# First batch's transposed q and k: where the four-way interleave is undone in the copy out of PSUM

## Chip, cores and metric

The kernel runs on one NeuronCore of a Trainium2 chip. The metric is device time of one execution in microseconds; of the kernel before, 13 runs gave a median of 309.38 us (307.45 to 310.54).

## What is computed

q, k and v have the shape (8 batches, 8 heads, 576 positions, 64). Per batch and head, retention: scores q k^T / 8, multiplied by a decay that is zero above the diagonal, times v. The heads are laid side by side (4608 tokens x 512) and go through a feed-forward block with a hard-swish, 512 to 2048 to 512.

```python
scores = scale * np.matmul(q, k.transpose(0, 1, 3, 2))
Dmat = np.where(rel >= 0, gamma[:, None, None] ** rel[None, :, :], 0.0)
attn = np.matmul(scores * Dmat[None], v)
x = np.ascontiguousarray(attn.transpose(0, 2, 1, 3)).reshape(B * S, H * D)
h = x @ w_in
out = (h * np.clip(h + 3.0, 0.0, 6.0) / 6.0) @ w_out
```

The decay is folded into q, k and v when they are cast to fp16 (tables `tq` and `tkv`), so that the scores need only a mask of zeros and ones.

## The kernel before

**Tiling.** A batch is cut into four chunks of 128 positions and a tail of 64; two tails make one more chunk. For each chunk: load q, k, v (`load`), cast them to fp16 with the decay (`cast`, L172), transpose q and k (`xpose`, by DMA, or `xpose_pe`, on TensorE), scores and mask (`ret1`: matmuls L277, VectorE's mask L284), then products with v, with the running state, and the new state (`ret2`: L300, L306, L325; ScalarE copies the result to `xt`, L330, and the state to fp16, L336). Four chunks fill `xt` for one batch. Then the up-projection (`up` L369, `up_half` L385) with the hard-swish (ScalarE L352, VectorE L357) and the down-projection: plain for batch 0 (`down_plain_part`, L412), by seven products of half size for the others (`product`, L483, with sums by VectorE, L447). Weights are loaded by `wload` (L539, L543) and cast by `wcast` (VectorE L555, ScalarE L557, GpSimd L559); `tbuild` (L572) makes differences of w_out.

**Order.** The order of the work is written out by hand in the string `PROGRAM`. Each engine runs its instructions in this order, and waits by semaphore for what others deliver. All loads and stores are issued by SP, in the same order; the DMA transposes are issued by ScalarE. The beginning reads

```
H19 L0.0 L0.1 L1.0 L1.1 C0.0v C0.1v V0 W0.0 W0.1 V1 V2 V3 W0.2 W0.3 c0.2g
C1.0v X0.0s W0.7 X0.1s X1.0s C1.1v X1.1s s0.4 K0v w0.0s s1 c1.2g K1v o0
```

H is 19 matmuls on zeros. L loads a half of the heads of q (0) or k (1); C casts it on VectorE; X transposes it, with the copy on ScalarE (the s at the end); V loads one chunk of v; W and w load and cast weights; c casts (on GpSimd, where the letter is g); s, o are `ret1`, `ret2`; K makes k back from its transpose; the second number of `s0.4` asks for four more matmuls on zeros.

**The first batch.** Its 512 positions take a way of their own. `load0` puts four neighbouring positions on one partition (partition p holds positions 4p to 4p + 3, 1024 bytes for each head), `cast0` (L208) casts them into `qk0["16"]` with r = 0 to 3 as the place among the four, and `xpose0` transposes, for each pair of heads a and each r, a block of 128 x 128 on TensorE (L223). A PSUM tile `tp` thus holds [pair, r, p]: positions r, 4 + r, 8 + r and so on. The attention needs them in order, 4p + r, and a copy (`copy`, ScalarE, L216) moves the tile into `wout16`, which serves as storage until w_out is cast into it. There are four such copies of 128 x 1024 fp16 elements: q heads 0 to 3, q heads 4 to 7, k heads 0 to 3, k heads 4 to 7. The scores of a chunk use all four: the first four matmuls of `ret1` use the first and the third copy, the last four the second and the fourth. `kback` transposes k of these chunks back (L237, copied by VectorE, L214), and `ret2` uses it for the state. The PSUM tiles of `xpose0` come from the four buffers with the tag `mm`, which the projections use later.

The functions around the change, and what calls them:

Of the kernel before, what the change touches and what calls it, by code (L numbers as in the profile page):

```python
# [83 lines left out]
def kernel(  # L84
# [39 lines left out]
    wout16 = const.tile([P, NFC, DM], FP16)  # L124
# [87 lines left out]
    def copy(eng, dst, src):  # L212
        if eng == "v":
            nc.vector.tensor_copy(dst, src)  # L214
        else:
            nc.scalar.copy(dst, src)  # L216

    def xpose0(ix, hh, eng):
        tp = psum.tile([P, 2, 4, P], FP16, tag="mm", bufs=4, name="tp")
        for a in range(2):  # L220
            for r in range(4):
                n0 = (2 * hh + a) * P
                nc.tensor.transpose(tp[:, a, r, :],  # L223
                                    qk0["16"][:, ix, r, n0:n0 + P], ident)
        p0 = 4 * ix + 2 * hh
        dst = wout16[:, p0:p0 + 2, :].rearrange("z a (p r) -> z a r p", r=4)
        copy(eng, dst, tp)
        if ix == 1 and hh == 1:
            for t in range(NC4):
                qkTs[(0, 0, t)] = wout16[:, 0:8, t * P:(t + 1) * P]  # L230
# [378 lines left out]
    for h in range(H):  # L609
        z = h % 2  # L610
# [17 lines left out]
    def act(w):  # L628
# [6 lines left out]
        elif kind == "C":  # L635
            cast0(*n, ENG[e])
        elif kind == "X":
            xpose0(*n, e)
        elif kind == "K":
            kback(*n, e)  # L640
# [65 lines left out]
```

## Time and profile before

The profiled execution took 310.37 us; its span is 308.2 us at a mean granted TensorE clock of 0.981.

| | us |
|---|---|
| median of 13 runs | 309.38 |
| profiled execution, span | 310.37, 308.2 |
| TensorE busy | 292.8 |
| VectorE, ScalarE, GpSimd busy | 241.9, 147.0, 108.8 |
| the four copies of `xpose0` (L216) | 9.3 in all |
| first start of L216, start of the second half of the first scores | 8.61, 17.92 |
| DMA, read and written | 36.70 MB, 9.44 MB |

An engine's row in a table of groups gives the busy time of the group, the mean duration of one instruction in ns, and then how long the engine sat idle just before these instructions and what it waited for. In the timeline the columns are start, duration, engine, line, operation, output and input, count, and in brackets the idle time before. In the chain of waits they are start, duration, and whose work the end hung on. In a row of the windows the stretch and its length come first, then each engine's busy time and instruction count (TensorE, its weight loads, VectorE, ScalarE, GpSimd), then the granted clock, the DMA share and the GB/s.

### The profile page before, as it was taken

How to read it: one execution, taken by the hardware profiler on the slowest of the kernel's cores; microseconds unless marked ns; L12 is line 12 of the kernel's file. 1: busy time of each engine (PE TensorE's matmuls, PEld its weight loads, DVE VectorE, ACT ScalarE, POOL GpSimd, SP SyncE). 2: the span in 40 equal slices, each digit the busy share in tenths (PEclk: the TensorE clock that was granted, in tenths of full speed). 3: DMA queues.
4: the chain of work that ended last, by engine and by line, in shares of the span. 5: the costliest groups of instructions: out<-in, count | busy, mean ns of one | idle time of the engine just before them, and what ended most of it. 6: DMA issues, size and time to landing. Idle time of an engine off the chain costs nothing.

```text
span 308.2 us, 7125 instructions
## 1 busy us (share of the span) xinstructions
PE 292.8 (95%) x2887; PEld 199.8 (65%) x2887; DVE 241.9 (78%) x335; ACT 147.0 (48%) x259; POOL 108.8 (35%) x120
## 2 busy tenths in 40 slices
PE   8369999989999999999999999999999999999995
PEld 3257445568788888746864686468655874685584
DVE  6346785988987989889877977898599767966963
ACT  2855762457235753366327522763277226505610
POOL 3164364894092655474375143332500000000000
PEclk9859999999999999999999999999999999999999
DMA  7999999999999999999999999989601430014003
GB/s 239 294 291 394 264 278 219 201 193 188 239 177 176 196 241 233 220 202 228 247 194 199 278 212 204 220 171 161 150 3 34 36 121 17 0 36 103 2 0 136
DMA packets 149728, 53.93 MB, mean 175 GB/s; under 512 B 134848, under 2 KB 145088, under 8 KB 149696
## 3 DMA queue, kind: packets, MB, share of 16 engines
q1 hardware_dynamic: 120128, 46.15, 68.2%
q10 hardware_dynamic: 29568, 7.34, 17.3%
q8 instruction: 22, 0.36, 0.5%
q14 instruction: 10, 0.08, 0.1%
HBM read 36.70 MB, written 9.44 MB: 150 GB/s over the span
## 4 chain that ended last, share of the span: by engine, by line
PE 85%; DVE 9%; ACT 4%; issue 1%; DVEq 0%
PE ph L369 29%; PE accB L483 9%; PE accC L483 9%; PE accA L483 9%; PE ph L385 8%; PE accD L483 5%; PE sc L277 4%; PE xp L300 4%; ACT wout L216 3%; PE xp L252 2%; PE po L412 2%; DVE g L357 2%; PE xp L306 2%; DVE tmat L572 2%; PE state L325 1%
## 5 line engine op out<-in xcount | busy, mean ns | idle before, releaser
L352 ACT ACTIVATE u<-ph 128x512 f32<-128x512 f32 x144 | 84.6, 597 | 67.2 <-PE ph L369 42.9
L357 DVE SCALAR_TENSOR_TENSOR g<-u,ph 128x512 f16<-128x512 f32 x144 | 95.3, 684 | 23.0 <-ACT u L352 21.4
L369 PE MATMUL ph<-xt,win 128*128 128x512 f16 x368 | 82.6, 379 | 0.2
L369 PEld LDWEIGHTS <-win 128*128 128x128 f16 x432 | 41.2, 98 | 48.3 <-DVE win L555 0.6
L483 PEld LDWEIGHTS <-ss 128*128 128x128 f16 x512 | 48.8, 98 | 7.1 <-DVE ss L447 1.1
L172 POOL TENSOR_TENSOR v<-st,tkv 128x512 f16<-128x512 f32 x31 | 35.2, 1142 | 46.4 <-DMA st<-in_v_dram 21.7
L284 DVE TENSOR_TENSOR at<-sc,mask 128x1024 f16<-128x1024 f32 x32 | 39.0, 1218 | 13.3 <-PE sc L277 13.2
L172 POOL TENSOR_TENSOR qk<-st,tq 128x512 f16<-128x512 f32 x29 | 31.8, 1096 | 41.2 <-PE state L325 24.0
L483 PEld LDWEIGHTS <-g 128*128 128x128 f16 x384 | 36.9, 98 | 5.5
L172 POOL TENSOR_TENSOR qk<-st,tkv 128x512 f16<-128x512 f32 x28 | 31.4, 1124 | 9.8 <-DMA st<-in_k_dram 9.0
L330 ACT ACTIVATE xt<-xp 128x512 f16<-128x512 f32 x32 | 19.1, 597 | 32.9 <-PE xp L306 20.6
L385 PE MATMUL ph<-xt,win 128*128 128x256 f16 x288 | 33.5, 273 | 1.1 <-DVE osb L420 1.1
L483 PE MATMUL accB<-tmat,ss 128*128 128x256 f16 x256 | 30.6, 273 | 0.2 <-DVE ss L447 0.2
L483 PE MATMUL accA<-wout,g 128*128 128x256 f16 x256 | 30.6, 273 | 0.0
L385 PEld LDWEIGHTS <-win 128*128 128x128 f16 x288 | 27.4, 98 | 4.9 <-issue 1.3
L447 DVE TENSOR_TENSOR ss<-g 128x1024 f16<-128x1024 f16 (+1 forms) x30 | 22.5, 754 | 0.3
L300 PE MATMUL xp<-at,v 128*64 128x128 f16 x288 | 20.3, 228 | 0.0
L300 PEld LDWEIGHTS <-v 128*64 128x64 f16 x288 | 14.2, 111 | 6.7 <-issue 3.4
L336 ACT CAST s<-state 64x256 f16<-64x256 f32 x48 | 17.3, 361 | 0.5
L503 ACT COPY osb<-accA 128x512 f32<-128x512 f32 x8 | 4.7, 586 | 23.9 <-PE accA L483 23.9
L412 PE MATMUL po<-wout,g 128*128 128x512 f16 x64 | 15.3, 379 | 0.6 <-DVE g L357 0.5
L483 PE MATMUL accC<-tmat,ss 128*128 128x256 f16 x128 | 15.4, 273 | 0.0
(87 smaller groups left out, 278.0 us busy)
## 6 DMA issues: line engine op xcount, KB each, us to landing
st<-in_v_dram SPq DMA_DIRECT2D x32, 256.0 KB, 6.0
out_dram<-osb SPq DMA_DIRECT2D x32, 256.0 KB, 3.7
st<-in_q_dram SPq DMA_DIRECT2D x28, 256.0 KB, 5.4
st<-in_k_dram SPq DMA_DIRECT2D x28, 256.0 KB, 5.4
wst<-in_moe_w_in_dram SPq DMA_DIRECT2D x4, 512.0 KB, 6.7
tmat<-in_moe_w_in_dram SPq DMA_DIRECT2D x4, 512.0 KB, 9.0
wst<-in_moe_w_out_dram SPq DMA_DIRECT2D x4, 512.0 KB, 10.5
g<-in_moe_w_out_dram SPq DMA_DIRECT2D x4, 512.0 KB, 8.1
```

Source lines behind the costliest of these rows:

```text
L172: eng.tensor_tensor(out=dst, in0=st[:, ix, :, :], in1=tab.unsqueeze(2).to_broadcast([P, H, D]), op=ALU.mult)
L284: nc.vector.tensor_tensor(out=at.rearrange("p z a i -> p (z a) i"), in0=sc.rearrange("p z a i -> p (z a) i"), in1=m[:, :].unsqueeze(1).to_ ...
L300: nc.tensor.matmul(xp[rows[z], p, :], vt[:, 2 * p + z, :], at[:, z, p, :], start=(p == 0), stop=False, skip_group_check=True)
L330: nc.scalar.activation(xts[b][:, :, t * P:(t + 1) * P], xp, ACTF.Copy, scale=0.125)
L336: nc.scalar.copy(s16[rows[z], :, rows[z]], sp[rows[z], :, :])
L352: nc.scalar.activation(u, ph, ACTF.Relu, bias=0.5, scale=1.0 / 6.0)
L357: nc.vector.scalar_tensor_tensor(out=dst, in0=uv, scalar=1.0, in1=pv, op0=ALU.min, op1=ALU.mult)
L369: nc.tensor.matmul(ph, win16[:, m, P * fc:P * fc + P], xt[:, m, :], start=(m == 0), stop=(m == NCC - 1))
L385: nc.tensor.matmul(ph[:, 256 * j:256 * j + 256], win16[:, m, P * fc:P * fc + P], xt[:, m, cs], start=(m == 0 and j == 0), stop=(m == NCC - 1),
L412: nc.tensor.matmul(po, g[:, fc, P * mc:P * mc + P], wout16[:, fc, :], start=(fc == 0), stop=(fc == NFC - 1))
L447: nc.vector.tensor_tensor(out=dst, in0=a, in1=c, op=op)
L483: nc.tensor.matmul(ps[:, m, :], lhs(fc, m), rhs[:, fc, :], start=(first and fc == 0 and m == 0), stop=(fc == HF - 1 and m == 1), skip_grou ...
```

## The change

The copy still moves the same 1024 elements a partition, on the same engine, at the same place in the program. Before, it read PSUM in the order in which it lies there, [pair, r, p], and wrote to SBUF with a step of four elements. After, it writes SBUF in the order in which that lies, [pair, p, r], and reads PSUM with r innermost, four elements that lie 128 elements apart.

```diff
         p0 = 4 * ix + 2 * hh
-        dst = wout16[:, p0:p0 + 2, :].rearrange("z a (p r) -> z a r p", r=4)
-        copy(eng, dst, tp)
+        dst = wout16[:, p0:p0 + 2, :].rearrange("z a (p r) -> z a p r", r=4)
+        copy(eng, dst, tp.rearrange("z a r p -> z a p r"))
```

## Prediction

> **What bounds the kernel now.** I read the page first, then the chain of waits in order of time, then the groups with shapes kept apart, then the timelines of TensorE and GpSimd over the first 30 us and of both TensorE and VectorE around 62 us, and last the windows for the granted clock.
>
> ```profile
> PE 292.8 (95%) x2887; PEld 199.8 (65%) x2887; DVE 241.9 (78%) x335; ACT 147.0 (48%) x259; POOL 108.8 (35%) x120
> PEclk9859999999999999999999999999999999999999
> ```
>
> TensorE is busy for 292.8 of 308.2 us. A change on another engine can win only from the 15.4 us in which TensorE idles, or from matmuls that run at a low granted clock, which the second row shows only in slices 2 and 3 (a slice is 7.7 us). The chain of waits names one large piece of that:
>
> ```profile
> 8.13 0.46 PE tp L223 x8
> 8.59 0.02 issue
> 8.61 9.26 ACT wout L216 x4
> 17.87 0.05 issue
> 17.92 0.41 PE sc L277 x4
> ```
>
> From 8.61 to 17.87 us the end hangs on four ScalarE copies in a row and on nothing else: the very copies that are changed. Then the scores of the first chunk start. TensorE's timeline shows when each copy could have started and what the wait costs:
>
> ```profile
> 9.89 0.62 PE L223 MATMUL tp<-ident,g 128*128 128x128 f16 x8 [0.87 <-DVE g L208]
> 11.39 0.62 PE L223 MATMUL tp<-ident,g 128*128 128x128 f16 x8 [0.88 <-DVE g L208]
> 11.85 0.39 PE L252 MATMUL sc<-zero 128*128 128x128 f16 x4
> 15.64 0.40 PE L277 MATMUL sc<-wout 64*128 64x128 f16 x4 [3.41 <-ACT wout L216]
> 17.92 0.40 PE L277 MATMUL sc<-wout 64*128 64x128 f16 x4 [1.88 <-ACT wout L216]
> ```
>
> The last transposes are done at 12.01 (11.39 + 0.62); the data is ready, and 3.41 + 1.88 = 5.29 us of idle TensorE are waits on L216. The groups give the price of such a copy, and of its nearest relative:
>
> ```profile
> L216 ACT COPY wout<-tp 128x1024 f16<-128x1024 f16 x4 | 9.3, 2512 | 6.0 <-PE tp L223 6.0
> L267 ACT COPY qkT<-tp 128x1024 f16<-128x1024 f16 x1 | 1.0, 1013 | 2.9 <-PE tp L263 2.9
> ```
>
> Same engine, same 1024 fp16 elements from PSUM to SBUF; L267 is contiguous on both sides and takes 1013 ns, L216 writes with a step of four elements and takes 2512 ns. So the step on the write costs 1.5 us per copy.
>
> **The change part by part.** The four copies keep their engine, place, count and semaphores. Removed: the stepped write. Added: a stepped read, four elements 128 apart (256 bytes), 256 runs of them. No DMA, wait, buffer or instruction is added or moved, so no queue (SP's and GpSimd's included) is passed; nothing new stands behind a wait.
>
> *Price of one new copy.* No row here reads PSUM with a step. Lower bound: the contiguous 1013 ns. The nearest row with a step is L216: 1499 ns extra on 1024 jumps, 1.46 ns a jump. Its jump is 8 bytes, the new one 256, and no row says how the price grows with the length; for the bound above I let it double, an assumption: 1013 + 1024 x 2.93 = 4.0 us. I take 1013 ns: the write becomes contiguous as in L267, only the reading side differs from that row, and at 1 ns an element L267 reads no faster than one element at a time, so that it draws little from reading neighbours. Both ends stay among the cases.
>
> [...]
>
> *The copy chain.* With 1.01 us each and starts no earlier than the transposes: first 8.61 to 9.62, second to 10.6; the third waits for transposes done at 10.51 and ends at 11.6; the fourth waits for 12.01 and ends at 13.04. Before: 17.87. So the second half of the first scores comes 4.83 us earlier; the four copies lose 6 us, 1.2 of which turn into waits for the casts L208 (paced by the k loads).
>
> *Where the gain meets a load.* What follows is an alternation of TensorE, VectorE and ScalarE, which moves up as a whole until it needs something that a load sets. First such place, GpSimd's timeline:
>
> ```profile
> 20.27 1.04 POOL L559 CAST win<-wst 128x1024 f16<-128x1024 f32 x1 [2.02 <-DMA wst<-in_moe_w_in_dram]
> 21.27 1.04 POOL L172 TENSOR_TENSOR v<-st,tkv 128x512 f16<-128x512 f32 x1
> ```
>
> The cast of the fourth v ends at 22.31 whatever ScalarE does, because the cast ahead of it in GpSimd's queue waits for a load; the products of the fourth chunk (ret2) cannot start before 22.35. They started at 27.12, so the gain is capped there at 4.77 us: any more that TensorE wins before is idled away. Next, the first full up-projection (31.82) waits for the VectorE cast L555, which stands behind an activation of the chunks before; it moves with the rest. Later loads: SP was blocked 7.0 us for that L555 (a staging buffer), yet the DMA queue ran at 387 GB/s until 31.8 and sagged only to 166 and 276 GB/s in the two us after, so later loads land about 0.9 us earlier, not 4.8. I therefore checked the casts against their users at 4.8 us less: k of chunk 5 is cast by 42.0, its transposes would come at 44.2; k of chunk 6 by 48.5 against 50.7; w_out part 4 by 44.7 against 47.3. Two us of slack remain at the tightest. From 65 us on SP waits again and again for buffers that the compute frees, so loads move with it. I cost these at nothing; if a slack were gone, up to 2 us would be lost.
>
> *What may be won besides.* VectorE is full from 55 to 65 us and TensorE stalls there:
>
> ```profile
> 63.24 1.03 PE L385 MATMUL ph<-xt,win 128*128 128x256 f16 x8 [1.15 <-DVE osb L420]
> 64.44 0.40 PE L277 MATMUL sc<-qkT 64*128 64x128 f16 x8 [0.17 <-DVE qkT L265]
> ```
>
> Between 0 and 1.32 us; VectorE's work there is still paced by loads that move only 0.9, so I take 0.4.
>
> *Clock.* The windows show it:
>
> ```profile
> 12.00:13.00 1.00, 0.23 (x5) 0.06 (x1) 0.00 (x0) 1.00 (x1) 0.41 (x1) 1.00 1.20 302
> 13.00:14.00 1.00, 0.00 (x0) 0.00 (x0) 0.00 (x0) 1.00 (x2) 0.00 (x0) 0.69 1.34 229
> 23.00:24.00 1.00, 1.00 (x25) 0.80 (x26) 0.39 (x1) 0.13 (x1) 0.00 (x0) 0.69 1.04 383
> ```
>
> It is halved from 13.4 to 23.6. With less idling it may stay up, or come back sooner (about 17); that gain lies ahead of the 22.35 cap, so it is worth 0. But the wait at that cap (about 1.2 us) thins TensorE's work between 20 and 23.6 to some 60%; 1.39 us busy in the 3.4 us before 13.37 brought a halving, 2.54 us in the 3.4 us before that did not. A halving there for 3.4 us would cost 1.7 us. I take 0.
>
> Sum: 4.8 + 0.4 = 5.2 us. The profiled execution took 310.37 us (span 308.2 and 2.2 around it), 1.0 above the median; from it 305.2, from the median of 309.38, 304.2.
>
> **Rivals.**
> 1. *The read costs as much as the write did, or the change moves the same penalty.* 2.5 us per copy, chain unchanged: 309.4. For it: both are one element per jump. Against: the 8-byte and 256-byte steps are on different memories.
> 2. *Something in between*, 1.76 us a copy (the midpoint of 1013 and 2512): the four run back to back, 8.61 + 4 x 1.76 - 0.3 = 15.4, 2.5 us gained: 306.9.
> 3. *Gain made, then partly eaten* by the halved clock at 23.6: 5.2 - 1.7 = 3.5: 305.9.
> 4. *Slower: a jump in PSUM costs 2.93 ns, twice one in SBUF.* 4.0 us a copy; the last ends at 8.61 + 16.0 - 0.3 = 24.3, 6.5 us late: 315.9. It decides from 2512 ns a copy on. Nothing in the trace excludes it.
> 5. *Hidden anyway*: later waits on loads give all back, 309.4. Against it: between 26 and 100 us TensorE idles only some 2.4 us in all, with casts ready 2 us and more ahead.
>
> **How the numbers follow.** Full-rate read and gain kept: 0.52, 302.9 to 305.5 (all of the 1.32 us stall and 0.1 more at the low end; 1.3 less at the high end). Rival 3: 0.15. Rival 2: 0.11. Rivals 1 and 5: 0.09. Rival 4 and lesser slow reads: 0.13. The range 302.9 to 309.4 leaves out the slow reads, half of the ties and the fringe: 2 in 10. A measurement of this kernel tells about 0.3% (0.9 us) from no change. Faster: 0.52 + 0.15 + 0.11 = 0.78; same 0.09; slower 0.13.
>
> **What would show it.** L216 near 1.0 us, the last copy's end near 13, first scores complete by 13.4, the fourth ret2 near 22.4 with a new TensorE wait on the v cast ahead of it, the first full up-projection near 27, less idle at 62. Wrong it would be by L216 over 2.5 us; or, with L216 at 1.0, by a new TensorE wait on a load-paced cast at 35 to 60 us, or a granted clock of 0.5 after 23.6.

## The result, and the profile after

The changed kernel takes 306.31 us (median of 11 runs, 305.47 to 307.09); the kernel before took 309.55 us in the 48 runs it is set against. The ratio is 0.9893 with a 95% interval of 0.9875 to 0.9912: faster by 3.2 us, or 1.1%. The forecast was 304.2 us, range 302.9 to 309.4. The sign and the price of the copy came out as forecast; 2.0 us of the forecast gain of 5.2 is missing, and most of what follows is about where it went.

Two rows of the page, busy time and, in 40 slices of 7.6 us, the granted TensorE clock:

```profile
PE 293.7 (96%) x2887; PEld 200.4 (66%) x2887; DVE 238.8 (78%) x335; ACT 141.5 (46%) x259; POOL 108.0 (35%) x120
PEclk9969999999999999999999999999999999999999
```

TensorE does the same 2887 matmuls and the span is 304.5 us instead of 308.2, so the gain is idle time that went; one slice instead of two is at a low clock. The group of the changed copies (the same columns as before):

```profile
L216 ACT COPY wout<-tp 128x1024 f16<-128x1024 f16 x4 | 4.0, 1013 | 7.3 <-PE tp L223 7.3
```

1013 ns instead of 2512, to the nanosecond the row of L267 that the prediction took. The four copies no longer run back to back: ScalarE now sits idle for 7.3 us ahead of them and waits for transposes. The chain of waits of the kernel after over the same stretch:

```profile
2.38 8.44 DMA g<-in_k_dram
10.82 0.02 issue
10.84 1.24 DVE g L208
12.08 0.05 issue
12.12 0.64 PE tp L223 x8
12.78 1.02 ACT wout L216
13.80 0.05 issue
13.85 0.41 PE sc L277 x4
```

Where 9.26 us of copies stood, one copy of 1.02 us is left. Ahead of it stands the load of the second half of k, issued at 2.38 us and landed at 10.82: in this execution the first scores are as early as that load lets them be. TensorE's timeline of the kernel after, past that point and around 62 us of the kernel before:

```profile
13.85 0.39 PE L277 MATMUL sc<-wout 64*128 64x128 f16 x4 [0.66 <-ACT wout L216]
...
23.44 0.25 PE L300 MATMUL xp<-at,v 128*64 128x128 f16 x2
...
27.45 9.12 PE L369 MATMUL ph<-xt,win 128*128 128x512 f16 x40
...
57.45 1.91 PE L385 MATMUL ph<-xt,win 128*128 128x256 f16 x16
59.30 0.40 PE L277 MATMUL sc<-qkT 64*128 64x128 f16 x8
```

Waits on L216 were 5.29 us and are 0.66. The products of the fourth chunk (ret2) start at 23.44 with no wait in brackets, the first full up-projection at 27.45, and the waits of 1.15 and 0.17 us ahead of the scores of chunk 7 are gone.

The starts of the same work in the two profiled executions show where the lead is won and lost (s7 is the scores of chunk 7, as in the written order):

| start of, us | before | after | lead | step |
|---|---|---|---|---|
| first scores, second half | 17.92 | 13.85 | 4.07 | won 4.07 |
| products of the fourth chunk | 27.12 | 23.44 | 3.68 | lost 0.39 |
| plain down-projection, second group | 43.64 | 40.04 | 3.60 | lost 0.08 |
| s7 | 64.44 | 59.30 | 5.14 | won 1.54 |
| s8 | 78.59 | 73.45 | 5.14 | |
| s9 | 85.22 | 81.02 | 4.20 | lost 0.94 |
| s13 | 104.86 | 100.67 | 4.19 | lost 0.01 |
| s15 | 117.48 | 113.80 | 3.68 | lost 0.51 |
| end of the span | 308.2 | 304.5 | 3.7 | |

From s15 to the end both take 190.7 us. So everything happens in the first 118 us: 4.1 us are won at the copies, 1.5 us at 62 us, and about 1.9 us are given back at four places. This is one pair of executions, whose spans differ by 3.7 us where the medians differ by 3.2. The experiments are about these steps.

### The profile page after: what moved, and what is told of

The parts are those of the page before. It is cut to its first block, busy times and chain, and to the rows that moved or that the text cites. A ratio compares the mean times of both kernels' runs of the same rounds, so it can differ in the third digit from the quotient of the medians.

```text
span 304.5 us, 7125 instructions
## 1 busy us (share of the span) xinstructions
PE 293.7 (96%) x2887; PEld 200.4 (66%) x2887; DVE 238.8 (78%) x335; ACT 141.5 (46%) x259; POOL 108.0 (35%) x120
## 4 chain that ended last, share of the span: by engine, by line
PE 87%; DVE 6%; DMA 3%; ACT 2%; issue 1%; SPq 0%; DVEq 0%; ACTq 0%
PE ph L369 30%; PE accB L483 10%; PE ph L385 9%; PE accC L483 8%; PE accA L483 8%; PE accD L483 5%; PE po L412 4%; PE xp L300 4%; PE sc L277 4%; DMA g<-in_k_dram 3%; DVE g L357 3%; DVE ss L447 2%; PE xp L306 2%; PE state L325 1%; ACT u L352 1%
## 5 line engine op out<-in xcount | busy, mean ns | idle before, releaser
L172 POOL TENSOR_TENSOR v<-st,tkv 128x512 f16<-128x512 f32 x31 | 33.8, 1095 | 51.2 <-DMA st<-in_v_dram 28.6
L284 DVE TENSOR_TENSOR at<-sc,mask 128x1024 f16<-128x1024 f32 x32 | 39.0, 1218 | 8.5 <-PE sc L277 8.4
L172 POOL TENSOR_TENSOR qk<-st,tq 128x512 f16<-128x512 f32 x29 | 31.6, 1091 | 34.2 <-PE state L325 14.8
L172 POOL TENSOR_TENSOR qk<-st,tkv 128x512 f16<-128x512 f32 x28 | 32.2, 1153 | 8.4 <-DMA st<-in_k_dram 8.1
L447 DVE TENSOR_TENSOR ss<-g 128x1024 f16<-128x1024 f16 (+1 forms) x30 | 22.7, 758 | 0.3
```

The source lines that it names most:

```text
L172: eng.tensor_tensor(out=dst, in0=st[:, ix, :, :], in1=tab.unsqueeze(2).to_broadcast([P, H, D]), op=ALU.mult)
L284: nc.vector.tensor_tensor(out=at.rearrange("p z a i -> p (z a) i"), in0=sc.rearrange("p z a i -> p (z a) i"), in1=m[:, :].unsqueeze(1).to_ ...
L447: nc.vector.tensor_tensor(out=dst, in0=a, in1=c, op=op)
```

## The experiments

**The two kernels once more.** Both without an edit, one more execution each, to see how much of the table above is one execution's chance.

> The changed kernel, one more look. In its first profile the first cast of k (L208) started at 9.33 us, 0.7 us later than in the profile of before (8.61), and so did every load of the first 30 us, although nothing has changed ahead of them. If the loads' pace is a chance of the execution, the first k cast starts anywhere from 8.6 to 9.4 here and the second half of the first scores follows it by 4.5 us; if the change makes the loads late, it starts at 9.3 again.

> The kernel before, one more look, for the same question. Chance: the first k cast starts anywhere from 8.6 to 9.4, while the second half of the first scores stays at 17.9 as long as the copies run back to back from 8.6 to 8.8 (the four copies hide a late k). Rival (the change makes the loads late): the first k cast starts at 8.6 again.

After: 306.05 us, span 303.9. Before: 311.82 us, span 309.7. The first scores' second half started at 13.47 and 16.94 us. The load of k moves by itself: its first cast started at 8.32 and 8.61 us in the two profiles of before, at 9.33 and 8.71 in those of after. The four pairings of these profiles put the lead at the first scores between 3.09 and 4.45 us. In the kernel before the scores came earlier than expected (17.9) because its first transposes began at 6.98 us instead of 7.96, and the four copies at 7.62 instead of 8.61. The half clock lasted 10.2 us in the first profile of before and 17.1 us in this one, and 6.8 us in both of after; with that the spans of the second pair differ by 5.8 us. The stall ahead of s7 was in both profiles of before (20.80 and 20.79 us from the second group of the plain down-projection to s7) and in neither of after (19.26 and 19.26).

**What a step costs, by itself.** Twenty-two copies of the same 1024 elements are added behind the end of the kernel, eleven on ScalarE and the same eleven on VectorE, each on a line of its own.

```diff
+    ts_ = tp.rearrange("z a r p -> z (a r p)")
+    tj = tp.rearrange("z a r p -> z a p r")
...
+    nc.scalar.copy(xa, ts_)
+    nc.scalar.copy(xq, tj)
+    nc.scalar.copy(x4, tp)
+    nc.scalar.copy(x2, ts_)
+    nc.scalar.copy(x8, ts_)
+    nc.scalar.copy(pr, tpr)
...
+    nc.scalar.copy(xa, s1)
+    nc.scalar.copy(xq, sj)
+    nc.vector.tensor_copy(xa, ts_)
+    nc.vector.tensor_copy(xq, tj)
+    nc.vector.tensor_copy(x4, tp)
...
```

> The changed kernel with 22 copies of 1024 elements added at its end, 11 on ScalarE and the same 11 on VectorE, each on a line of its own; its time is not to be read. Theory: reading PSUM with a jump is free on ScalarE, and the price of the old copy belongs to writing single fp16 elements with a step. Then ScalarE: contiguous 1.01 us; read jumping 256 bytes 1.01; write with a step of 4 elements 2.5, of 2 and of 8 elements also about 2.5 (a half-word written alone costs the same wherever it lies); pairs of fp16 with a step 1.0; fp32 written with steps of 2 and 4 1.0. Rival: the price grows with the distance: step 2 about 1.7, step 4 2.5, step 8 more, pairs in between, and stepped fp32 dearer than contiguous fp32. [...]

Groups by line of that kernel. L698 and L709 are contiguous on both sides, L699 and L710 read PSUM with the change's jumps, L700 and L711 write every fourth fp16, L702 and L713 every eighth:

```profile
L702 ACT COPY win<-tp 128x1024 f16<-128x1024 f16 x1 | 4.7, 4681 | 0.0
L713 DVE COPY win<-tp 128x1024 f16<-128x1024 f16 x1 | 4.7, 4680 | 0.0
...
L700 ACT COPY win<-tp 128x1024 f16<-128x1024 f16 x1 | 2.4, 2420 | 0.0
L711 DVE COPY win<-tp 128x1024 f16<-128x1024 f16 x1 | 2.4, 2420 | 0.0
...
L710 DVE COPY win<-tp 128x1024 f16<-128x1024 f16 x1 | 1.2, 1224 | 0.0
...
L698 ACT COPY win<-tp 128x1024 f16<-128x1024 f16 x1 | 1.0, 1012 | 5.1 <-PE tp L681 5.1
L699 ACT COPY win<-tp 128x1024 f16<-128x1024 f16 x1 | 1.0, 1012 | 0.0
...
L709 DVE COPY win<-tp 128x1024 f16<-128x1024 f16 x1 | 0.7, 691 | 18.5 <-ACT win L708 18.5
```

| 1024 elements, ns | ScalarE | VectorE |
|---|---|---|
| PSUM to SBUF, contiguous | 1012 | 691 |
| PSUM read with jumps of 256 bytes | 1012 | 1224 |
| fp16 write, step of 2, 4, 8 elements (4, 8, 16 bytes) | 1291, 2420, 4681 | 1291, 2420, 4680 |
| fp16 write in pairs, a pair every 8 bytes | 1012 | 693 |
| fp32 write, contiguous, step of 2, 4 (8, 16 bytes) | 1012, 1055, 1951 | 1224, 1224, 1950 |
| SBUF to SBUF, contiguous and read with jumps | 1044, 1911 | 427, 1253 |

On ScalarE the jumps in PSUM cost nothing (1012 ns in L699 as in L698); VectorE's copy goes from 691 to 1224 ns with them. The stepped fp16 write costs the same on both engines (2420 ns at a step of four elements), though these differ by 1.5 times without a step (1012 and 691), which points to the receiving side and not to the engine. It nearly doubles with each doubling of the step (1291, 2420, 4681). It isn't a price per jump: pairs of fp16 at the same 8 bytes are free (1012 and 693). So the flat price that the theory expected is wrong and growth with the step, the rival, is right, but pairs are free as the theory had it.

**Half of the change.** q is copied as before, k as after.

```diff
+        if ix == 0:
+            dst = wout16[:, p0:p0 + 2, :].rearrange("z a (p r) -> z a r p", r=4)
+            copy(eng, dst, tp)
+        else:
...
```

> Half of the change: the two copies of q write with a step as before, the two of k read with a jump as after. The first two copies then take 2.5 us each, the k copies follow without a gap, and the last one ends at about 8.7 + 2 x 2.45 + 2 x 0.95 = 15.5 instead of 13.0 to 13.8 (after) and 17.9 (before). Theory that a gain at the first scores passes to the end one for one: 2.4 us better than before, so 307.1. Rival, that loads cap the gain near 3.2 us whatever the start is: nearly the whole of 3.2 us already here, 306.5. Rival, that half a gain is worth nothing because the clock or a later stall takes it: 309.

Its copies in the groups of that kernel:

```profile
L216 ACT COPY wout<-tp 128x1024 f16<-128x1024 f16 x4 | 6.5, 1774 | 6.0 <-PE tp L223 6.0
```

306.95 us, ratio 0.9899 (0.9846 to 0.9951). The mean copy is what the prediction's second rival assumed (1.76 us), and the median is near what it gave (306.9). That agreement proves little: the ratio makes it 306.4 where the kernel before takes 309.55, and its interval runs from 304.8 to 308.0. Of the three cases expected, only the last, 309, is excluded.

Against the profiled execution of the full change it is 1.21 us later at the first scores (15.06 against 13.85), but only 0.57 at the state of the fourth chunk (24.67 against 24.10), 0.29 at s7 and 0.2 at the end. In both the clock is halved for 6.83 us, but full speed is granted again at 20.05 us in it and at 20.6 in the full change, while the work stands 1.21 us later: more of it runs at full speed. In these two executions the last 1.21 us of lead at the first scores are worth 0.2 us at the end.

**The clock kept up.** More matmuls on zeros fill TensorE's waits between 8 and 18 us; the copies are the changed ones.

```diff
-C1.0v X0.0s W0.7 X0.1s X1.0s C1.1v X1.1s s0.4 K0v w0.0s s1 c1.2g K1v o0
+C1.0v X0.0s W0.7 X0.1s H4 X1.0s H3 C1.1v X1.1s s0.12 K0v H3 w0.0s s1 c1.2g K1v o0
```

> The changed kernel with more matmuls on zeros in TensorE's idle time between the transposes and before the first two chunks' scores (10 of 512 columns and 8 of 128), so that the clock is not halved between 12 and 20 us. If it works, the work from the first scores to the fourth chunk's products, 9.6 us in both profiles of after (13.85 to 23.44 in one), takes about 1.8 us less. Theory, that the loads then take over: the third quarter of the up-projection needs the cast of a w_in piece that ends at 29.2 to 30.9 us, and TensorE already comes there at 29.9 to 30.9, so the end gains 0.7 us at most: 306.0 against 306.3 for after. Rival, that the half clock is what still holds the start: 1.8 us gained, 304.5.

The mean granted clock is 1.0 in the profile, and the fourth chunk's products meet the wait that the prediction had put there. TensorE's timeline of that kernel:

```profile
21.32 0.25 PE L300 MATMUL xp<-at,v 128*64 128x128 f16 x2 [0.74 <-POOL v L172]
```

The v cast ends at 21.27 and the products start, 2.12 us ahead of the changed kernel's 23.44. But most of that isn't the clock's. The loads came earlier in this execution: the second cast of k started at 9.59 us instead of 10.84, so that the first scores were complete 1.19 us sooner (12.66 against 13.85), and the fourth v cast ended at 21.27 instead of 23.04. From these scores to the products it takes 8.66 us instead of 9.59, 0.93 less where 1.8 was expected, because the wait for the cast takes 0.74. Had the cast ended at 23.04 here too, at most 0.4 us would have been won. Whether the added matmuls have a part in the earlier loads, no run shows. In that profile the lead holds: 2.16 us at s7, 2.3 in the span (302.2). But it doesn't hold from one execution to the next: the four times are 304.66, 306.72, 307.74 and 308.63, median 307.23, ratio 0.9894 (0.9847 to 0.9942), which decides between neither of the two expectations. The clock was 0.994 or more in all four, so that what the later ones lost they lost elsewhere; only the first has a profile, and this stays open.

**The stall at 77 us.** In the changed kernel TensorE waits 0.87 us for a sum `ss` there, and in the kernel before it doesn't. VectorE's timeline of the kernel before, and then that of the kernel after, over the same work:

```profile
76.55 0.71 DVE L447 TENSOR_TENSOR ss<-g 128x1024 f16<-128x1024 f16 x1
...
77.78 1.28 DVE L572 TENSOR_TENSOR tmat<-wout 128x1024 f16<-128x1024 f16 x2
```

```profile
71.41 1.41 DVE L447 TENSOR_TENSOR ss<-g 128x1024 f16<-128x1024 f16 x1
...
73.34 1.53 DVE L572 TENSOR_TENSOR tmat<-wout 128x1024 f16<-128x1024 f16 x2
```

The same instructions took 0.95 us longer. GpSimd was idle from 76.71 to 85.43 us in the kernel before; in the kernel after it casts beside them, and TensorE waits (GpSimd's timeline before, GpSimd's after, then TensorE's after):

```profile
75.67 1.04 POOL L172 TENSOR_TENSOR v<-st,tkv 128x512 f16<-128x512 f32 x1 [0.18 <-DMA st<-in_v_dram]
85.43 1.78 POOL L172 TENSOR_TENSOR qk<-st,tq 128x512 f16<-128x512 f32 x1 [8.71 <-PE state L325]
```

```profile
70.23 2.04 POOL L172 TENSOR_TENSOR v<-st,tkv 128x512 f16<-128x512 f32 x2
72.49 1.23 POOL L172 TENSOR_TENSOR qk<-st,tq 128x512 f16<-128x512 f32 x1 [0.22 <-DMA st<-in_q_dram]
```

```profile
77.44 1.05 PE L483 MATMUL accC<-tmat,ss 128*128 128x256 f16 x8 [0.87 <-DVE ss L447]
78.70 1.92 PE L483 MATMUL accB<-tmat,ss 128*128 128x256 f16 x16 [0.21 <-DVE ss L447]
```

GpSimd's casts are paced by loads (the bracket), which did not move with the compute: the k of chunk 12 is cast at 74.45 us in the kernel before and at 74.75 in the kernel after, while the scores of chunk 8 come 5.14 us earlier. VectorE now meets casts that it did not meet before. A first attempt moves a v cast forward in GpSimd's order, out of the way:

```diff
-c9.2g l15 c10.0g c10.1g c11.0g c11.1g c10.2g x8 h1.0.4.12 h1.0.5.13 o7 x9
+c9.2g l15 c10.0g c10.1g c10.2g c11.0g c11.1g x8 h1.0.4.12 h1.0.5.13 o7 x9
```

> The changed kernel with one GpSimd cast moved: the v of the eleventh load is cast ahead of the q and k of the twelfth, which wait for their loads. In after, these casts fall on VectorE's first sum for the fast products (L447, 1.41 us instead of 0.71, at 71.4) and TensorE idles 0.87 us at 77. Theory (this collision gives back a part of the gain): L447 near 0.7 us, no wait of 0.87 at 77, 0.9 us gained: 305.4. Rival (VectorE is behind there for other reasons, or the collision only moves to its neighbour): 306.3 as after.

306.62 us, ratio 0.9891 (0.9859 to 0.9923): the collision only moved. L447 took 1.14 us, and the wait was 0.71 us.

A second moves v casts back, behind those of the next chunk:

```diff
-c9.2g l15 c10.0g c10.1g c11.0g c11.1g c10.2g x8 h1.0.4.12 h1.0.5.13 o7 x9
+c9.2g l15 c10.0g c10.1g c11.0g c11.1g x8 h1.0.4.12 h1.0.5.13 o7 x9
...
-t2 h1.1.5.13 c11.2g l16 x10 l17 c12.0g c12.1g h1.1.6.14 c12.2g h1.1.7.15
+t2 h1.1.5.13 c12.0g c12.1g c10.2g c11.2g l16 x10 l17 h1.1.6.14 c12.2g h1.1.7.15
```

> The changed kernel with the casts of v of chunks 10 and 11 put behind the casts of q and k of chunk 12 in GpSimd's order: the same work, two casts of it later. If the collision costs the time and the casts can be placed beside work that does not mind, the wait for ss at 77 us shrinks to 0.2 us and the median falls by 0.5 us or more. Rival: q of chunk 12 waits for its load, all casts behind it slide into the later sums (L447, L492) at 77 to 81 us, another wait takes the place of this one, and the median is within 0.3 us of the changed kernel or above it.

306.35 us, ratio 0.9901 (0.9867 to 0.9935). The rival was right: L572 is back at 1.28 us, but the first sum still meets a k cast (1.47 us), the two later sums are stretched too (1.12 and 1.95 us), and the waits are 1.12 and 0.94 us, more than ever; behind s9 a third follows, of 1.06 us.

A third leaves three casts out: their v and q are filled with zeros.

```diff
+        if (order.index(c), ix) in ((10, 2), (11, 2), (12, 0)):
+            eng.memset(dst, 0.0)
+            eng.tensor_tensor(out=dst[:, 0, 0:8], in0=st[:, ix, 0, 0:8],
+                              in1=tab[:, 0:1].to_broadcast([P, 8]),
+                              op=ALU.mult)
+            return
```

> The changed kernel without the three GpSimd casts that run beside VectorE's L447 and L572 from 70 to 74 us (v of chunks 10 and 11, q of chunk 12): each is replaced by a fill with zeros and a cast of 8 elements, so the work of these casts is left out. If the collision of the two engines costs the time, L447 takes 0.7 us and L572 1.28 us there, the wait for ss ahead of accC at 77 us is gone, and the median is 0.6 to 0.9 us under the changed kernel. Rival: those operations are slow for another reason, or something behind them is late in any case; then the wait stays at 0.8 us, or it goes and the median stays within 0.3 us.

Its VectorE timeline (its lines are six higher: L453 is L447, L578 is L572), GpSimd's beside it, and TensorE's:

```profile
70.84 0.69 DVE L453 TENSOR_TENSOR ss<-g 128x1024 f16<-128x1024 f16 x1
...
72.05 1.30 DVE L578 TENSOR_TENSOR tmat<-wout 128x1024 f16<-128x1024 f16 x2
...
75.35 1.13 DVE L453 TENSOR_TENSOR ss<-g 128x1024 f16<-128x1024 f16 x1
76.51 1.95 DVE L453 TENSOR_TENSOR ss<-ss,g 128x2048 f16<-128x2048 f16 x1
```

```profile
70.87 0.53 POOL L173 MEMSET v<- 128x512 f16 x1
...
74.89 1.04 POOL L178 TENSOR_TENSOR qk<-st,tkv 128x512 f16<-128x512 f32 x1 [2.09 <-DMA st<-in_k_dram]
75.89 1.49 POOL L178 TENSOR_TENSOR v<-st,tkv 128x512 f16<-128x512 f32 x1
```

```profile
76.53 1.05 PE L489 MATMUL accC<-tmat,ss 128*128 128x256 f16 x8 [0.53 <-DVE ss L453]
78.52 1.92 PE L489 MATMUL accB<-tmat,ss 128*128 128x256 f16 x16 [0.94 <-DVE ss L453]
```

With the casts gone the first sum takes 0.69 us, beside a fill, and the differences 1.30: the casts are the cause of the stretch, and the fill doesn't stretch the sum. But the next k was loaded only by 74.89 us, and its cast and the one behind it hit the two following sums (1.13 and 1.95 us). The time is 306.53 us, ratio 0.9912 (0.9882 to 0.9942): nothing was gained, against what the first theory had expected. The loads still decide which sum is hit.

The changed kernel beside these runs shows the same from the other side:

> The changed kernel again, as the base for the three runs beside it. About 306.3 us, 3.2 us under the kernel before. TensorE's wait for the sum ss ahead of accC near 77 us is there again, 0.8 to 0.9 us, with one L447 of 1.4 us and a stretched L572 ahead of it on VectorE.

306.04 us, ratio 0.9885 (0.9861 to 0.9909), as expected; but in the execution that was profiled the wait was 0.16 us and not 0.8. There the first sum started at 70.81 us and took 0.69, and GpSimd's q cast, which started at 70.82, was the one stretched (1.58); only L572 was slow (1.54). Over the profiles, the work from s7 to s9 against the waits of TensorE ahead of accC and accB (less the 0.21 us ahead of accB that the kernel before has too) (the row of half of the change and the last four are kernels of the other experiments):

| us | s7 to s9 | above before | waits above before |
|---|---|---|---|
| before | 20.78 | | |
| before, once more | 21.09 | 0.31 | 0.23 |
| changed, beside the last runs | 21.01 | 0.23 | 0.16 |
| changed | 21.72 | 0.94 | 0.87 |
| changed, once more | 21.89 | 1.11 | 0.89 |
| half of the change | 21.61 | 0.83 | 0.76 |
| v cast moved forward | 21.57 | 0.79 | 0.71 |
| v casts moved back | 22.70 | 1.92 | 1.85 |
| three casts out | 22.11 | 1.33 | 1.26 |
| clock kept up | 22.13 | 1.35 | 1.11 |
| weight casts moved | 21.49 | 0.71 | 0.64 |
| weight casts moved, once more | 21.43 | 0.65 | 0.56 |
| all three edits | 21.49 | 0.71 | 0.72 |

The delay is the wait, within 0.1 us in all rows but two (0.22 and 0.24). So it is shown that the casts stretch these sums, and the loss at this place is TensorE's wait for them; no run removed the wait. Its size is drawn anew in each execution, between 0.2 and 1.1 us for the changed kernel and 0 and 0.3 for the kernel before.

The same kind of collision lies ahead of the gain at 62 us. VectorE's timeline of the kernel before ahead of that stall, then that of the kernel after:

```profile
54.95 1.52 DVE L172 TENSOR_TENSOR v<-st,tkv 128x512 f16<-128x512 f32 x1
56.40 0.68 DVE L172 TENSOR_TENSOR qk<-st,tq 128x512 f16<-128x512 f32 x1
57.00 1.53 DVE L172 TENSOR_TENSOR qk<-st,tkv 128x512 f16<-128x512 f32 x1
58.45 3.00 DVE L572 TENSOR_TENSOR tmat<-wout,tmat 128x1024 f16<-128x1024 f16 x2
61.38 1.21 DVE L284 TENSOR_TENSOR at<-sc,mask 128x1024 f16<-128x1024 f32 x1
```

```profile
51.60 0.68 DVE L172 TENSOR_TENSOR v<-st,tkv 128x512 f16<-128x512 f32 x1
52.26 0.69 DVE L172 TENSOR_TENSOR qk<-st,tq 128x512 f16<-128x512 f32 x1
53.29 0.69 DVE L172 TENSOR_TENSOR qk<-st,tkv 128x512 f16<-128x512 f32 x1 [0.34 <-DMA st<-in_k_dram]
53.90 2.13 DVE L572 TENSOR_TENSOR tmat<-wout,tmat 128x1024 f16<-128x1024 f16 x2
55.96 1.21 DVE L284 TENSOR_TENSOR at<-sc,mask 128x1024 f16<-128x1024 f32 x1
```

Three casts and two differences took 6.73 us and now take 4.19. GpSimd was casting in the kernel before from 53.20 to 55.94 and from 56.48 on, most of its casts stretched as well (1.28 to 1.50 us instead of 1.04); in the kernel after it waits for a load from 51.13 to 54.36. That VectorE was full there before was true, but over a third of these 6.73 us (2.54) is what the same five instructions took beyond their 4.19 us in the kernel after. That this is why the stall went is read from the profiles (both of before have the 3.0 us, none of after); no run was made to test it by itself.

**Weight casts moved.** In the changed kernel ScalarE waits 0.61 us at 33 us for the load of a weight that it casts, and TensorE at 37 and 39 us 0.18 and 0.20 us for VectorE's `g`, which stands behind it. Here three weight casts change places, and the v cast of the fourth chunk goes ahead of a weight cast (the second expectation below counts four weight casts and speaks of a k cast; the edit is the same).

```diff
-w0.1g s2.8 o1 s3 c2.2g w0.2g o2 h0.0.0.1 W0.4 c3.2g o3 W0.5 h0.0.2.3 w0.3v
-W1.0 h0.1.0.1.8 W1.6 W0.6 W1.7 W1.1 W1.2 w0.5g h0.1.2.3 W1.3 l4 l5 W1.4 W1.5
-u0.4 u0.5 u0.6 l6 w0.7g u0.7 w0.4g u0.8 w1.7s u0.9 l7 w0.6g w1.3g w1.6v
-c4.0g u0.10 w1.0s u0.11 u0.12 u0.13 u0.14 u0.15 w1.1g c4.1v c5.0g p0 y4v l8
+w0.1g s2.8 o1 s3 c2.2g c3.2g w0.2g o2 h0.0.0.1 W0.4 o3 W0.5 h0.0.2.3 w0.3v
+W1.0 h0.1.0.1.8 W1.6 W0.6 W1.7 W1.1 W1.2 w0.7g w0.4g w0.5g h0.1.2.3 W1.3 l4 l5 W1.4 W1.5
+u0.4 u0.5 u0.6 l6 u0.7 u0.8 u0.9 l7 w0.6g w1.3g w1.6v
+c4.0g u0.10 w1.0s u0.11 u0.12 u0.13 u0.14 u0.15 w1.7s w1.1g c4.1v c5.0g p0 y4v l8
```

> The changed kernel with the early casts in the order in which their loads land and are needed: the fourth v ahead of a w_in piece, the last w_in piece of the third quarter behind two that have landed before it, and a w_out cast of ScalarE (which waits 0.61 us for its load in the middle of the activations) moved behind the up-projection. Theory: in after none of these casts is what TensorE waits for except the last, which costs it 0.38 us in the up-projection; so 306.0, and the start stays bound by its own chain at half clock. Rival, that the order of these casts is the cap as I predicted: 1 to 2 us gained, 304.8.

> The changed kernel with four weight casts and the fourth k cast moved in the order of the work, again and beside the changed kernel. Theory one, the earlier run was right: about 305.3, 1.0 us under the changed kernel, because the waits of the up-projection for w_in at 33 us are gone and nothing takes them back. Rival, the gain is taken back by the same wait for ss at 77 us: within 0.4 us of the changed kernel.

305.25 us, ratio 0.9839 (0.9807 to 0.9872), and beside the changed kernel 305.17 us, ratio 0.9875 (0.9837 to 0.9914), where that took 306.04. The medians lie 1.1 and 0.9 us under the changed kernel's, but drawing again and again from the two lists of times of the last call puts the difference between -1.2 and +0.9 us: it points to a gain, as theory one of the second expectation has it (305.3), and doesn't settle it. The profile of the second run shows what can take it back. VectorE's timeline of that kernel, in the stretch in which the changed kernel lost 0.51 us:

```profile
105.90 1.45 DVE L447 TENSOR_TENSOR ss<-g 128x1024 f16<-128x1024 f16 x1
...
109.18 0.69 DVE L447 TENSOR_TENSOR ss<-g 128x1024 f16<-128x1024 f16 x1
109.90 1.95 DVE L447 TENSOR_TENSOR ss<-ss,g 128x2048 f16<-128x2048 f16 x1
```

Two more sums are stretched beside casts (104.67 to 106.80, and from 109.45), TensorE waits 0.47 and 0.94 us, and from s9 to s15 the kernel needs 34.01 us (the kernel before 32.26, the changed kernel 32.78). This execution took 306.65 us, the slowest of its six.

**All three edits together**: the matmuls on zeros, the v cast moved forward, and the weight casts.

> The changes of the three kernels above together. If the clock, the casts' order and the collision are what is left at the start, they add up here although the first two give little alone: 1.8 us from the start, 0.4 from the up-projection, 0.9 at 77, so 303.2. Rival, that later loads set the pace whatever the start does (half of the change gave all but 0.6 us of the whole one's gain): 305.4, only the collision's share.

306.38 us, ratio 0.9880 (0.9839 to 0.9921): the parts don't add up to 303.2. At 57 us its profile is 2.7 us ahead of the changed kernel's (1.43 of them at the first scores, where the k load was early again); s7 to s9 loses 0.71 us against before, and at 130 us a wait for `g` of 1.43 us takes more: the span is 303.1, 1.4 us less than the changed kernel's.

## Right and wrong, by the prediction's own steps

- **The price of the copy: right.** 1013 ns in the kernel, 1012 against 1012 side by side. Its reason, that L267 reads one element at a time, was the author's estimate from 1 ns an element, and no run shows how many are read at once; the runs show that the jumps left ScalarE's copy at 1012 ns and took VectorE's from 691 to 1224, 533 more.
- **The chain of copies, 4.83 us: mis-sized, 4.07.** The step from copies to transposes to casts to the k load was as worked out. But the sum took the k load as fixed, and it was 0.72 us later in the profiled execution. Over the profiles its first cast starts between 7.9 and 9.3 us. The end of the copies is now as uncertain as that load.
- **The cap at the fourth v cast: right as a place, not reached in the profiled execution.** The cast ended at 23.04 (the load ahead of it in GpSimd's queue had come 0.73 us later), and the products started at 23.44. 0.39 us of the lead was lost ahead of them: the second chunk's products ran wholly at half clock and took 0.86 us up to the state's matmuls instead of 0.51, so that the third chunk's products waited for ScalarE's copies of the state. In two other profiles the fourth products did wait for the cast: 0.74 us with the clock kept up, 0.26 with the v casts moved back, where the edit comes much later.
- **The clock, costed at 0: too low by 0.4 us at most in the profiled execution.** Full speed was granted at 20.6 us and not at 17. The reason given, that the cap takes what the clock gives, fits the run with the clock kept up: there TensorE waits at the cap, and between the end of the changed kernel's own cast and its products lie only 0.40 us (0.66 and 0.79 in its two other profiles), which is the most that the clock could have won. The time over four executions shows no gain either. The second halving (rival 3) didn't come: the clock is 1.0 from 20.6 us on. Its 1.7 us was the author's estimate, half of a halving of 3.4 us. The profiled halvings lasted 6.8, 10.2 and 17.1 us, near 2, 3 and 5 times that; one execution of the changed kernel (306.11 us, span 303.9, mean clock 0.994) had some 3.6 us at half clock, estimated as 2 x 0.006 x 303.9.
- **The stall at 62 us, taken as 0.4: mis-sized, 1.54.** The upper bound of 1.32 us was nearer. The reason given for the small value, that VectorE there is paced by loads, is not what the profiles show: it was stretched by GpSimd's casts, and those fell elsewhere (not tested by itself).
- **Later loads cost nothing: the step that failed.** It asked whether each cast would be ready for its user, and found 2 us of slack; in the profile of the changed kernel TensorE waits for no cast of q, k or v after 24 us. What it did not ask is what a load-paced cast does to the engine beside it while it runs. 0.94 us went at 77 us this way in the profiled pair, and 0.6 us on the mean of three profiles of the changed kernel against two of the kernel before. A further 0.51 us went between s13 and s15: there ScalarE's issue of a DMA transpose took 2.44 us instead of 1.81, and the activation behind it and VectorE's sum were late. This is read from the two profiles and was not tested, and it need not come from the change: the same stretch took 12.62 and 13.08 us in the two profiles of the kernel before, 13.13, 13.37 and 13.31 in three of the changed kernel.

The profiled pair adds up: 5.2 forecast, less 0.76 (k load), less 0.39 and 0.08 (to 43 us), plus 1.14 (62 us), less 0.94 (77 us), less 0.51 (by s15) and 0.02 between, is 3.64; the spans differ by 3.7.

Of the rivals, the first and the fourth fall with the price of the copy. The second gave 306.9 for a copy at half the penalty, the third 305.9 for a second halving of the clock. The measured 306.31 lies between the two by chance, for the copy paid no penalty and no second halving came. The fifth, that later waits take the gain back, was right in part, by a mechanism that it didn't name. That the sum came within 2.1 us is thus partly luck: more was won at 62 us than the sum had, and more was lost at 77. What would have made the prediction wrong in its own words was a TensorE wait on a load-paced cast; the new wait is on a sum that such casts had slowed.

## What to carry to other kernels

When the copy that undoes an interleave goes from PSUM to SBUF on ScalarE, put the step on the PSUM read and write SBUF in order: 2512 ns became 1013 for 1024 fp16 elements. When compute is moved ahead of loads, look not only at whether each cast is in time, but at what the load-paced engine will then run beside: list VectorE's sums, differences and casts from SBUF to SBUF within the shift (here L447, L572, L172) and GpSimd's casts; where they met here, a VectorE instruction took up to 0.7 to 0.9 us longer (a sum L447 0.69 to 1.57 us, a cast L172 0.68 to 1.53). A lead won at the start also changes which of them meet; measure it at several later points before counting on it.

## What the runs showed of the hardware

- A stepped fp16 write to SBUF cost 1291, 2420 and 4681 ns for 1024 elements at 4, 8 and 16 bytes, the same on ScalarE and VectorE within 1 ns, while pairs at 8 bytes were free (1012 and 693, without a step 1012 and 691). fp32 at 8 bytes was nearly free (1055 on ScalarE, without a step 1012; 1224 on VectorE as without a step) and cost 1951 and 1950 at 16 bytes.
- A jumping read of PSUM was free on ScalarE (1012 with and without) and took VectorE from 691 to 1224; a jumping read of SBUF cost both (1044 to 1911, 427 to 1253).
- VectorE's L447, L572 and L172, with two inputs in SBUF, were stretched by up to 0.7 to 0.9 us an instruction where they met a GpSimd cast (L447 0.69 to 1.41 and once 1.57, with twice the elements 1.22 to 2.06; L172 0.68 to 1.53; two of L572 1.28 to 1.53, and in the kernel before 3.00), and the casts too (1.04 to 1.58, in both kernels also 2.02, at 88 us before and at 84 us after). L555, a weight cast with one input in SBUF, took 0.69 us alone and 1.40 beside a GpSimd cast (30.37 us before). L284, with one input in PSUM, took 1.21 to 1.23 us beside casts or not. The one sum beside a GpSimd fill wasn't stretched either (0.69).
- With the copies in the way the clock was halved for 10.2 and 17.1 us in two executions, with the change for 6.8 us in two and with half of it for 6.83 us in one; with more matmuls on zeros the mean granted clock was 1.0 and 0.999 in two.
